# Block-sorted attention with a max-out layer behind it: the opening and the second batch's sorts in another order

## The chip, the cores and the metric

One core of one Trainium2 chip runs the whole program. The metric is the device time of one execution in microseconds (us); every number below is from the kernel before the change.

## What is computed

Inputs are q, k and v of shape 4 x 8 x 768 x 64 (batch, head, position, width), a sorting net of 4 x 8 x 8 x 8, and three weight matrices. Cut to what matters, the reference is:

```python
for _ in range(5):                       # Sinkhorn: P becomes a soft permutation of 8 blocks
    P = exp(P - max(P)); P /= sum(P, -1); P /= sum(P, -2)
k_sorted = einsum('bhij,bhjcd->bhicd', P, k_blocks)     # blocks of 96 positions
v_sorted = einsum('bhij,bhjcd->bhicd', P, v_blocks)
attn = softmax(q_blocks @ k_sorted.T / 8)               # inside each block
x = (attn @ v_sorted) as 3072 tokens x 512
out = maximum(x @ w1, x @ w2) @ w_out                   # d_ff = 1024
```

## The kernel before

**Stages.** The 32 Sinkhorn problems are done once, in small operations of VectorE (DVE) and ScalarE (ACT), while TensorE (PE) multiplies zeros (`keep_streaming`, line 77; the opening's call is line 666). The result is laid out as block-diagonal matrices (`block_diagonals`, line 293). Then, for each of the four batches:

- `sort_k` (line 385, three calls for a batch) and `sort_v` (line 409, four calls) multiply raw keys and values with those matrices; each has 16 or 32 small products in one PSUM tile, and one evacuation to SBUF. For batches 0 and 1 the values are first put into another order by `turn_v` (line 209, calls by columns 0 to 96), on ACT or DVE.
- `q_transposes` (line 349), in two halves. For batches 0 and 1 this is done by PE, for batches 2 and 3 by transposing DMAs of SyncE's queue (SP), after `pair_q` (line 339, DVE) has paired the heads. Half 0 holds head pairs 0 and 1, half 1 pairs 2 and 3.
- `scores` u = 0 to 7 (line 452): eight products and the exponential on ACT. u = 4·(half of the blocks) + head pair, so u = 0, 1, 4, 5 read q's half 0, and 2, 3, 6, 7 half 1.
- `values` u (line 480): eight products on PE, then on DVE a reciprocal (line 499) and a scaling (line 505) that writes x.
- `x_transposes` t = 0 to 3 (line 513), named TR in the text: t covers u = 2t and 2t + 1. For batch 0 it is done by PE and evacuated (`eng` says by which engine); for the other batches it is a transposing DMA on SP (line 518).
- the feed-forward layer: w1 is replaced by w1 - w2 in four column pieces (`w_difference`), since max(h1, h2) = relu(h1 - h2) + h2; `moe_h` (line 598) makes the relu part in eight steps for a batch, of which steps 0 to 3 read TR 0 and 1 and steps 4 to 7 read TR 2 and 3; within a step the head pairs come in the order 0, 2, 1, 3, and pairs 1 and 3 read the odd TR. `w2_transposes` and `w_product` make w2·w_out once. `moe_out` (line 627) makes the output for 128 tokens in two parts; after each second group of tokens one evacuation (128 x 1024 fp32) and one 512 KB write on SP.

**Order.** All engines run their instructions in the order in which the program issues them. The opening up to batch 0's attention is written out by hand (lines 666 to 722). Then a loop over batches runs a list of units (for batch 0: four `moe_h` of the first half, of which two are already done, four of the second, four `w_product`, twelve `moe_out` parts: units 0 to 23). After unit n it issues `tail[n]` (a table of extra steps by unit, lines 732 to 742), and then some of `steps`, the sorts and the attention of the next batch, spread from unit `lo` on in proportion to the units' costs. An evacuation without a named engine goes to ACT or DVE by `pick` (line 96), which keeps a running sum of the work given to each.

**Buffers and queues.** PSUM holds four tiles in rotation for everything; a product waits until one is free. All loads are issued by GpSimd's queue (POOL) with a cast from fp32 to bf16; q's raw tile has one buffer, so a load of q waits until the transposes or `pair_q` of the batch before have read it. Batch 2's load stands in `tail[14]`, batch 3's behind `pair_q(2)` in `tail[18]` (line 741).

Of the kernel before, what the change touches and what calls it, by code (L numbers as in the profile page):

```python
# [16 lines left out]
def kernel(  # L17
# [21 lines left out]
    B, H, S, D = q.shape  # L39
# [26 lines left out]
    def ps_f32(name):  # L66
        return psum.tile([128, 1024], FP32, tag="ps", name=name)

    def ps_bf16(name):
        return psum.tile([128, 2048], BF16, tag="ps", name=name)  # L70
# [6 lines left out]
    def keep_streaming(ps, n, by=None, most=512):  # L77

        w0 = fill[:, 0:128] if by is None else late[by]
        while n > 0:  # L80
            w = min(n, most)
            nc.tensor.matmul(ps[:, 0:w], w0, fill[:, 0:w], start=True, stop=True)  # L82
            n -= w
# [43 lines left out]
    for n in range(NE):  # L127
        t = big.tile([BLK, 8 * BLK + 32], BF16, tag=f"e{n}", name=f"e{n}")
# [16 lines left out]
    def load_k(b):  # L145
        k_raw[b] = kpool.tile([128, HB * D], BF16, tag="k_raw", name="k_raw")
        n = HB * D // NCH
        for ci in range(NCH):
            nc.gpsimd.dma_start(
                out=k_raw[b][:, ci * n : (ci + 1) * n],  # L150
                in_=k_src[b, :, ci * n : (ci + 1) * n],
            )

    def load_v(b, c0=0, pieces=2):
        r0 = (b % 2) * 64
        n = (BLK - c0) * D // pieces
        for m in range(pieces):
            nc.gpsimd.dma_start(
                out=v_raw[r0 : r0 + 64, c0 * D + m * n : c0 * D + (m + 1) * n],
                in_=v_src[b, :, c0 * D + m * n : c0 * D + (m + 1) * n],  # L160
            )
# [30 lines left out]
    def w_difference(t, eng=None):  # L192
        n = DFF // 4
        (eng or nc.vector).tensor_tensor(  # L194
            out=w1_sb[:, :, t * n : (t + 1) * n],
            in0=w1_sb[:, :, t * n : (t + 1) * n],
            in1=w2_sb[:, :, t * n : (t + 1) * n],
            op=ALU.subtract,
        )
        if not eng:  # L200
            load["D"] += 600

    w_difference(0, nc.gpsimd)
    w_difference(1, nc.gpsimd)
    load_v(1)
    load_k(1)


    def turn_v(rows, eng, c0, c1):
# [139 lines left out]
    def q_transposes(b, half, eng=None):  # L349

        if half == 0:
            qT[b] = qpool.tile([128, HP, R, 128], BF16, tag="qT", name="qT")
        if b > 1:
            hps = slice(half * 2, half * 2 + 2)
            nc.sync.dma_start_transpose(
                out=qT[b][:, hps].rearrange("p h r c -> p (h r) c"),
                in_=q_pair[b][:, hps].rearrange("p h r d -> p (h r d)"),
            )
            return
        ps = ps_bf16("tq_ps")  # L360
        if b == 0:
            nc.tensor.matmul(
                ps[:, 0:128], fill[:, 0:128], ident, is_transpose=True, start=True, stop=True
            )
        for n in range(2 * R):
            hp, r = half * 2 + n // R, n % R
            c = slice(n * 128, (n + 1) * 128)
            for h2 in range(2):
                nc.tensor.matmul(  # L369
                    ps[h2 * 64 : h2 * 64 + 64, c],  # L370
                    q_raw[b][:, hp + 4 * h2, r * D : (r + 1) * D],
                    ident,
                    is_transpose=True,
                    start=True,
                    stop=True,
                )
        evac(
            qT[b][:, half * 2 : half * 2 + 2].rearrange("p h r c -> p (h r c)"),
            ps[:, 0 : 2 * R * 128],
            2 * R * 128,  # L380
            two_x=True,
            eng=eng,
        )
# [274 lines left out]
    def att(b):  # L658

        SC = [lambda u=u: scores(b, u) for u in range(8)]  # L660
        VA = [lambda u=u: values(b, u) for u in range(8)]
        TR = [lambda t=t: x_transposes(b, t) for t in range(4)]
        return SC, VA, TR

    first, second, both = slice(0, 64), slice(64, 128), slice(0, 128)
    keep_streaming(ps_f32("fill_ps"), 88 * 138, most=138)
    for it in range(5):
        sinkhorn(it)
        if it < 2:
# [9 lines left out]
    turn_v(first, "D", 80, 96)  # L679

    SC, VA, TR = att(0)
    sort_k(0, 0, 2048, "A")
    sort_k(0, 1, 0, "D")
    sort_k(0, 2, 0, "A")
    sort_v(0, 0, 0, "D")
# [2 lines left out]
    sort_v(0, 2, 0, "A")  # L688
    sort_v(0, 3, 0, "D")
    SC[0]()  # L690
    SC[1]()
    q_transposes(0, 1, "D")
    SC[4]()
    VA[0]()
    scores(0, 2, 1024)
    VA[1]()
    SC[3]()
    values(0, 2, 1024)
    x_transposes(0, 0, "A")
    values(0, 3, 512)  # L700
    SC[5]()
    moe_h_products(0, 0, 0, (0, 2), 512)
    x_transposes(0, 1, "A")
    VA[4]()
    SC[6]()
    moe_h(0, 0, 0, "A", (1, 3))
    SC[7]()
    VA[5]()
    moe_h(0, 0, 1, "A")
    x_transposes(0, 2, "A")  # L710
    VA[6]()
    w_difference(2)
    VA[7]()
    w2_transposes(0, "D")()
    w_difference(3)
    for b in range(1, B):
        selections(b)
    for c, n, m in [(2, 1, 0), (3, 3, 1)]:
# [5 lines left out]
    def turn(rows, c0):  # L724
        turn_v(rows, "D", c0, c0 + 24)
        load["D"] += 850

    def load_rest():
# [1 line left out]
        load_k(2)  # L730

    tail = {
        2: [TR[3], lambda: w2_transposes(1, "A")(), load_rest],
        4: [lambda: turn(second, 0)],
        5: [lambda: block_diagonals([(0, 2), (1, 1), (1, 2), (1, 3)], 2)],
        6: [lambda: turn(second, 24), lambda: turn(second, 48)],
        7: [lambda: turn(second, 72)],
        8: [lambda t=t: sort_k(1, t) for t in range(3)],
        9: [lambda: load_v(2), lambda: load_v(3), lambda: load_k(3)],
        14: [lambda: load_q(2)],  # L740
        18: [lambda: pair_q(2, 0), lambda: pair_q(2, 1), lambda: load_q(3)],
# [1 line left out]
    for b in range(B):  # L743
        units = [lambda t=t: moe_h(b, 0, t, None if b else "A") for t in range(4)]
        if b == 0:
            units[0] = lambda: None
            units[1] = lambda: None
        units += [lambda t=t: moe_h(b, 1, t) for t in range(4)]
        cost = [13] * 8
        if b == 0:  # L750
            units += [lambda dmt=dmt: w_product(dmt) for dmt in range(4)]
            cost += [17] * 4
        units += [
            lambda ti=ti, part=part: moe_out(b, ti, part)
            for ti in range(6 if b < B - 1 else 4)
            for part in range(2)
        ]
        cost += [13] * 12
        if b == B - 1:
            units += [  # L760
                lambda: moe_out_last(4, [(0, 512, "D")]),
                lambda: moe_out_last(5, [(0, 384, "D"), (384, 512, "A")]),
            ]
        steps, lo = [], 0
        if b < B - 1:
            qs = [lambda half=half: q_transposes(b + 1, half) for half in range(2)]
            ks = [lambda t=t, b=b: sort_k(b + 1, t) for t in range(3)]
            SC, VA, TR = att(b + 1)

            def group(*fs):  # L770
                return [lambda: [f() for f in fs]]

            if b == 0:
                lo = 9
                vs = [lambda t=t: sort_v(1, t) for t in range(4)]
                for m, c in enumerate((0, 24, 48, 72)):
                    VA[m + 1 : m + 2] = group(VA[m + 1], lambda c=c: turn(both, c))
                steps = group(*vs[0:2]) + group(vs[2], qs[0]) + group(vs[3], qs[1])
            elif b == 1:
                vs = [lambda t=t: sort_v_pair(2, t) for t in range(8)]  # L780
                tail[0] = qs
                tail[10] = [lambda: pair_q(3, 0), lambda: pair_q(3, 1)]
                steps = group(*ks) + group(*vs[0:2]) + group(*vs[2:4]) + group(*vs[4:6])
                steps += group(*vs[6:8])
            else:
                tail[0] = qs
                lo = 4
                steps = group(*ks)
            steps += group(*SC[0:2]) + VA[0:1] + group(*SC[2:4]) + VA[1:2] + group(VA[2], TR[0])
            steps += group(*SC[4:6]) + VA[3:4] + group(VA[4], TR[1]) + group(*SC[6:8]) + VA[5:6]  # L790
            steps += group(VA[6], TR[2]) + group(VA[7], TR[3])
        done = 0
        for n, unit in enumerate(units):
            elapse(100 * cost[n] if n < len(cost) else 0)
            unit()
            for step in tail.get(n, []):
                elapse(250)
                step()
            total = sum(cost[lo:])
            want = -(-len(steps) * sum(cost[lo : n + 1]) // total)  # L800
            while done < min(want, len(steps)):
                elapse(250)
                steps[done]()
                done += 1
        tail = {}
# [28 lines left out]
```

## Time and profile before

| what | us |
|---|---|
| median of 3 runs (170.62 to 171.14) | 171.06 |
| the profiled execution | 170.89 |
| its span, first to last instruction | 169.0 |
| outside the span | 1.89 |
| PE busy | 161.8 |
| ACT busy | 85.8 |
| DVE busy | 75.8 |
| GpSimd busy | 28.6 |

The span lists PE, DVE and ACT work with start times; "busy" of PE includes the products of zeros. A waiting instruction shows the idle time before it and what released it. q0 is the queue of the loads that GpSimd issues, q1 that of the DMAs that SP issues (output writes and transposes). "To landing" is the time from a DMA's issue until all its data are in place.

Some matmul records are missing from the trace (a group of 8 is then shown as "x5" or "x7"), and the gap that this leaves is shown as "issue".

### The profile page before, as it was taken

What the parts mean: (1) busy time and instruction counts of PE and PEld (TensorE: products, weight loads), DVE (VectorE), ACT (ScalarE), POOL (GpSimd) and SP (SyncE); (2) the same over time, 40 slices, a digit from 0 to 9 for tenths busy, and PEclk for the clock granted to TensorE, in tenths of its full rate; (3) what the DMA queues carried; (4) which work ended last, traced back from release to release, by engine and by line L of the source; (5) the groups of instructions that cost most, each with busy time, mean ns of one, the idle gap of its engine ahead of it and who ended that gap; (6) DMA issues with size and microseconds to landing.
All of it is one profiled execution on the core that took longest, in us unless ns stands there. A gap on an engine that the chain in (4) does not pass through costs nothing.

```text
span 169.0 us, 4526 instructions
## 1 busy us (share of the span) xinstructions
PE 161.8 (96%) x2000; PEld 97.9 (58%) x2018; DVE 75.8 (45%) x174; ACT 85.8 (51%) x104; POOL 28.6 (17%) x44
## 2 busy tenths in 40 slices
PE   7999999999999999999999999999999999999991
PEld 7949676755764454566564545557545456654451
DVE  5968864948464459437743433205442160000011
ACT  3587878474674353176674505456615416642020
POOL 7865585223312003000000000000000000000000
PEclk9999999999999999999999999999999999999999
DMA  3999999999999994999700253690053255000333
GB/s 46 202 205 197 199 207 206 224 197 206 216 221 200 205 230 82 186 148 232 160 0 4 66 151 134 98 288 16 0 36 139 50 169 175 0 0 0 124 146 106
DMA packets 30243, 23.11 MB, mean 137 GB/s; under 512 B 16720, under 2 KB 25168, under 8 KB 30224
## 3 DMA queue, kind: packets, MB, share of 16 engines
q0 software_dynamic: 10880, 12.59, 44.8%
q1 hardware_dynamic: 19200, 10.17, 24.9%
q8 instruction: 16, 0.26, 0.6%
q10 hardware_dynamic: 144, 0.07, 0.1%
q14 instruction: 3, 0.02, 0.0%
HBM read 25.17 MB, written 6.29 MB: 186 GB/s over the span
## 4 chain that ended last, share of the span: by engine, by line
PE 92%; DVE 3%; issue 2%; ACT 1%
PE out_ps L617 35%; PE h_ps L590 25%; PE fill_ps L82 6%; PE o_ps L488 4%; PE wc_ps L570 4%; PE k_ps L394 4%; PE s_ps L461 4%; PE v_ps L415 2%; PE tq_ps L369 2%; PE v_ps L436 1%; PE tx_ps L526 1%; ACT v_sb L108 1%; DVE qT L110 1%; PE k_ps L82 1%; DVE q_pair L343 1%
## 5 line engine op out<-in xcount | busy, mean ns | idle before, releaser
L617 PE MATMUL out_ps<-wo_sb,g 128*128 128x512 bf16 (+2 forms) x188 | 47.0, 370 | 1.1 <-issue 0.3
L590 PE MATMUL h_ps<-xT,w_sb 128*128 128x384 bf16 x256 | 44.7, 326 | 0.6 <-ACT xT L108 0.4
L590 PEld LDWEIGHTS <-w_sb 128*128 128x128 bf16 x256 | 24.0, 98 | 16.4 <-DVE w_sb L194 0.4
L108 ACT COPY o<-out_ps 128x1024 f32<-128x1024 f32 x11 | 11.1, 1012 | 40.4 <-issue 22.8
L604 ACT ACTIVATE g<-h_ps 128x768 bf16<-128x768 f32 x27 | 21.9, 812 | 16.7 <-PE h_ps L590 16.7
L469 ACT ACTIVATE e<-s_ps 96x768 bf16<-96x768 f32 x32 | 24.2, 804 | 6.3 <-PE s_ps L461 6.3
L617 PEld LDWEIGHTS <-g 128*128 128x128 bf16 x200 | 16.9, 97 | 15.7 <-DVE x L505 0.4
L617 PE MATMUL out_ps<-wc,xT 128*128 128x512 bf16 (+2 forms) x100 | 24.8, 370 | 0.1
L505 DVE TENSOR_TENSOR x<-o_ps,rs 96x512 bf16<-96x512 f32 x32 | 22.0, 686 | 1.1
L499 DVE RECIPROCAL rs<-o_ps 96x8 f32<-96x8 f32 x32 | 6.5, 202 | 34.0 <-PE o_ps L488 33.8
L617 PEld LDWEIGHTS <-xT 128*128 128x128 bf16 x100 | 9.6, 97 | 11.2
L488 PEld LDWEIGHTS <-e 96*128 96x128 bf16 x256 | 11.7, 98 | 6.0 <-ACT e L469 0.2
L488 PE MATMUL o_ps<-v_sb,e 96*128 96x65 bf16 x256 | 12.9, 193 | 0.0
L652 DVE COPY o<-out_ps 128x512 f32<-128x512 f32 (+1 forms) x2 | 1.2, 625 | 25.0 <-PE out_ps L617 25.0
L110 DVE CAST kT<-k_ps 128x1024 bf16<-128x1024 f32 x5 | 6.0, 1223 | 12.3 <-PE k_ps L394 12.3
L110 DVE CAST v_sb<-v_ps 96x1024 bf16<-96x1024 f32 x8 | 9.6, 1216 | 2.8 <-PE v_ps L415 1.7
L461 PEld LDWEIGHTS <-kT 64*128 64x128 bf16 x256 | 6.1, 94 | 6.2 <-issue 5.4
L108 ACT CAST v_sb<-v_ps 96x1024 bf16<-96x1024 f32 x8 | 8.0, 1006 | 3.2 <-PE v_ps L415 1.9
L136 POOL DMA_DIRECT2D q_raw<-in_q_dram x7 | 6.4, 936 | 18.7 <-DVE rs L499 14.0
L82 PEld LDWEIGHTS <-fill 128*128 128x128 bf16 x98 | 8.5, 122 | 1.6 <-DVE fill L73 1.2
L461 PE MATMUL s_ps<-qT,kT 64*128 64x96 bf16 x256 | 8.9, 204 | 0.4 <-DVE qT L110 0.2
L82 PE MATMUL fill_ps<-fill 128*128 128x138 bf16 x88 | 7.9, 274 | 1.2 <-DVE fill L73 1.2
(77 smaller groups left out, 137.5 us busy)
## 6 DMA issues: line engine op xcount, KB each, us to landing
out_dram<-o SPq DMA_DIRECT2D x11, 512.0 KB, 3.1
k_raw<-in_k_dram POOLq DMA_DIRECT2D x12, 256.0 KB, 12.2
v_raw<-in_v_dram POOLq DMA_DIRECT2D x6, 384.0 KB, 12.5
q_raw<-in_q_dram POOLq DMA_DIRECT2D x3, 768.0 KB, 11.5
w_sb<-in_moe_w_dram POOLq DMA_DIRECT2D x4, 256.0 KB, 9.9
w_sb<-in_moe_w_dram POOLq DMA_DIRECT2D x2, 512.0 KB, 11.2
wo_sb<-in_moe_w_out_dram POOLq DMA_DIRECT2D x2, 512.0 KB, 14.9
v_raw<-in_v_dram POOLq DMA_DIRECT2D x3, 256.0 KB, 4.9
```

Source lines behind the costliest of these rows:

```text
L82: nc.tensor.matmul(ps[:, 0:w], w0, fill[:, 0:w], start=True, stop=True)
L108: nc.scalar.copy(out=out_ap, in_=in_ap)
L110: nc.vector.tensor_copy(out=out_ap, in_=in_ap)
L394: nc.tensor.matmul(ps[r0 : r0 + 64, m * 64 : (m + 1) * 64], kv[r0 : r0 + 64, t * 16 + m, :], bd_k[b][r0 : r0 + 64, :], start=True, stop=True,)
L461: nc.tensor.matmul(ps[:, h2 * 512 + ii * 128 : h2 * 512 + ii * 128 + BLK], kT[b][rows, (hp * 8 + i) * BLK : (hp * 8 + i) * BLK + 128], rhs ...
L469: nc.scalar.activation(out=e[:, 0 : 8 * BLK].rearrange("p (t c r) -> p t c r", t=8, r=R), in_=ps[0:BLK] .rearrange("p (t f) -> p t f", t=8 ...
L488: nc.tensor.matmul(ps[:, h2 * 512 + ii * 65 : h2 * 512 + (ii + 1) * 65], e[:, (h2 * 4 + ii) * BLK : (h2 * 4 + ii) * BLK + 128], v_sb[:, m0 ...
L505: nc.vector.tensor_tensor(out=x, in0=ov[:, :, :, 0:D], in1=rs.to_broadcast([BLK, 2, 4, D]), op=ALU.mult,)
L570: nc.tensor.matmul(ps[:, 0:512], w2T[:, fb, dmt * 128 : (dmt + 1) * 128], wo_sb[:, fb, :], start=(fb == 0), stop=(fb == NFB - 1),)
L590: nc.tensor.matmul(h_ps[t][:, m * 512 : m * 512 + TCH], w1_sb[:, hp, fb * 128 : (fb + 1) * 128], xT[:, b % 2, ch, hp % 2, hp // 2, :], sta ...
L604: nc.scalar.activation(out=g, in_=src, func=AF.Relu)
L617: nc.tensor.matmul(dst, g_tiles[b, ch, m // 2][:, m % 2, off : off + 128] if m < NFB else xT[:, b % 2, ch, hp % 2, hp // 2, off : off + 12 ...
```

## The change

It has two groups of edits.

In the opening: q's half 1 is transposed directly behind `scores` 0 instead of behind `scores` 1; `scores` 4 moves from behind them to behind `x_transposes(0, 0)`; the second `x_transposes` is evacuated by DVE instead of ACT; `values` 5 stands ahead of `scores` 7; `w_difference(3)` stands ahead of the evacuation of the first `w2_transposes`. The zero products ahead of `sort_k(0, 0)` go from 2048 columns to 1024, ahead of `scores` 2 from 1024 to 512; one product of zeros ahead of q's half 1 goes; the opening's 88 products of 138 columns become 86 of 142.

In the second batch: its keys are loaded ahead of its values; its three `sort_k` move from `tail[8]` to `tail[7]` with fixed engines and with the value turns between and behind them; its `sort_v` and `q_transposes` leave `steps` for `tail[9]` to `tail[11]`; `lo` goes from 9 to 12, so `steps` begins with `scores` 0 and 1. The second `w2_transposes` and the loads of `load_rest` move from `tail[2]` to `tail[3]`.

```diff
-    load_v(1)
     load_k(1)
+    load_v(1)
...
-        if b == 0:
+        if b == 0 and half == 0:
...
-    keep_streaming(ps_f32("fill_ps"), 88 * 138, most=138)
+    keep_streaming(ps_f32("fill_ps"), 86 * 142, most=142)
...
-    sort_k(0, 0, 2048, "A")
+    sort_k(0, 0, 1024, "A")
...
     SC[0]()
+    q_transposes(0, 1, "D")
     SC[1]()
-    q_transposes(0, 1, "D")
-    SC[4]()
     VA[0]()
-    scores(0, 2, 1024)
+    scores(0, 2, 512)
     VA[1]()
     SC[3]()
     values(0, 2, 1024)
     x_transposes(0, 0, "A")
+    SC[4]()
     values(0, 3, 512)
     SC[5]()
     moe_h_products(0, 0, 0, (0, 2), 512)
-    x_transposes(0, 1, "A")
+    x_transposes(0, 1, "D")
     VA[4]()
     SC[6]()
     moe_h(0, 0, 0, "A", (1, 3))
+    VA[5]()
     SC[7]()
-    VA[5]()
...
-    w2_transposes(0, "D")()
+    w2T_ready = w2_transposes(0, "D")
     w_difference(3)
+    w2T_ready()
...
     tail = {
-        2: [TR[3], lambda: w2_transposes(1, "A")(), load_rest],
-        4: [lambda: turn(second, 0)],
+        2: [TR[3]],
+        3: [lambda: w2_transposes(1, "A")(), load_rest],
         5: [lambda: block_diagonals([(0, 2), (1, 1), (1, 2), (1, 3)], 2)],
-        6: [lambda: turn(second, 24), lambda: turn(second, 48)],
-        7: [lambda: turn(second, 72)],
-        8: [lambda t=t: sort_k(1, t) for t in range(3)],
+        7: [
+            lambda: sort_k(1, 0, 0, "A"),
+            lambda: turn(second, 0),
+            lambda: turn(second, 24),
+            lambda: sort_k(1, 1, 0, "A"),
+            lambda: sort_k(1, 2, 0, "D"),
+        ],
+        8: [lambda: turn(second, 48), lambda: turn(second, 72)],
         9: [lambda: load_v(2), lambda: load_v(3), lambda: load_k(3)],
         14: [lambda: load_q(2)],
         18: [lambda: pair_q(2, 0), lambda: pair_q(2, 1), lambda: load_q(3)],
...
             if b == 0:
-                lo = 9
+                lo = 12
...
-                steps = group(*vs[0:2]) + group(vs[2], qs[0]) + group(vs[3], qs[1])
+                tail.update({9: vs[0:2] + tail[9], 10: [vs[2], qs[0]], 11: [vs[3], qs[1]]})
```

More of the change, by code (lines that the diff above doesn't have):

```diff
@@ L204 @@
     w_difference(1, nc.gpsimd)
+    load_k(1)
     load_v(1)
-    load_k(1)
     def turn_v(rows, eng, c0, c1):
```

## Prediction

> **What bounds the kernel now.** I read the busy line and the chain first, then the waits of PE, then the opening, then SP's queue against the loads.
>
> ```profile
> PE 161.8 (96%) x2000; PEld 97.9 (58%) x2018; DVE 75.8 (45%) x174; ACT 85.8 (51%) x104; POOL 28.6 (17%) x44
> PE 92%; DVE 3%; issue 2%; ACT 1%
> ```
>
> PE is the bound and its work is in a fixed order, so only three things change the time: products of zeros, waits of PE, and new waits. The waits of PE between 12 and 72.6 us (engine, line, releaser: total, times, longest):
>
> ```profile
> PE h_ps L590 <- ACT xT L108: 0.4, 1, 0.4
> PE out_ps L617 <- DVE x L505: 0.3, 1, 0.3
> PE h_ps L590 <- DVE w_sb L194: 0.3, 1, 0.3
> PE s_ps L461 <- DVE qT L110: 0.2, 1, 0.2
> ```
>
> From 72.6 us to the end the same view lists none. So there is about 1.2 us of waits to win, and some zeros. In the opening, q's half 1 arrives late and scores 2 wait for it (timeline: start, duration):
>
> ```profile
> 18.34 0.86 PE L369 MATMUL tq_ps<-ident,q_raw 128*64 128x128 bf16 x24
> 19.24 0.96 DVE L110 COPY qT<-tq_ps 128x1536 bf16<-128x1536 bf16 x1 [0.42 <-PE tq_ps L369]
> 20.25 0.60 PE L461 MATMUL s_ps<-qT,kT 64*128 64x96 bf16 x8 [0.21 <-DVE qT L110]
> ```
>
> Now batch 1's TR, which the change delays. SP's queue (TR 1 at 64.11; TR 2 and 3 from 69.36), POOL's load of q for batch 3, and how long a DMA took to land: TR 1 took 2.8 us, TR 2 8.6 us.
>
> ```profile
> 64.11 1.22 SPq L518 DMA_TRANSPOSE xT<-x  x1
> 67.03 0.38 SPq L637 DMA_DIRECT2D out_dram<-o  x1
> 69.36 4.80 SPq L518 DMA_TRANSPOSE xT<-x  x2
> 66.07 1.77 POOL L136 DMA_DIRECT2D q_raw<-in_q_dram  x1 [13.99 <-DVE rs L499]
> xT<-x SPq DMA_TRANSPOSE x1, 2.8
> xT<-x SPq DMA_TRANSPOSE x1, 8.6
> ```
>
> The reason for 8.6 us is in the packets between 71 and 74 us: q0 (the load) moves, q1 (SP's DMAs) all but stands still.
>
> ```profile
> q0 software_dynamic: 626, 0.48, 120.1%
> q1 hardware_dynamic: 22, 0.01, 1.5%
> ```
>
> The first q0 packets of that load come in the slice from 69 us, about 3 us after its issue; it lands after 11.5 us, at 77.6; TR 2 lands at 69.36 + 8.6 = 78.0, just behind it. Nobody needs TR 2 before 81.9, so this costs nothing now.
>
> **What the Trainium skill says.** "DMA: Bandwidth & Descriptors", section "Queues, rings and completion order", says that a DMA engine takes turns between the queues, one packet each, and that one queue's descriptors go in order on each engine. The trace is harsher on the first point (626 packets to 22), and agrees with the second as far as it shows. Even fair turns would not help: the load has about 1,010 packets, a transpose about 800, so it would take most of the load's 7.5 us. "TensorE: Matmul & The Clock Gate", section "Part 1: The HAM clock gate", says that PE's clock halves after an idle window of some 3.4 us. No wait in this trace is that long; it bears on one rival below.
>
> **The change, part by part.**
>
> *Zeros.* Four products of 512 ahead of sort_k 0 become two: 4 x 0.21 us run from 11.80 to about 12.66, but the block diagonal ends near 12.73 and the sort starts at 12.83. So at most 0.05 us is won; I take 0.05. The zero product ahead of q's half 1 goes (0.06, inside the next sum). 86 x 142 against 88 x 138 columns is 0.6% of a 7.9 us row: 0 to +0.05 us, taken as 0.
>
> *q's half 1.* Behind scores 0 (one set is 0.27 us, from 17.58) its transposes run 17.84 to 18.63, since they take the PSUM tile that half 0's copy left at 17.53. DVE is busy with the last value sort to 18.82, then copies (0.96) to 19.78, not 20.20. Scores 2 start at 19.83: 0.42 us earlier. But scores 4 (0.27 us) filled that wait and now run later, and one zero product less (0.21) had filled it too, so behind values 3 PE is only 0.15 us ahead. Values 0 and scores 1 fit without a wait; counting tiles against their releases I find a free one each time.
>
> *TR 1 of batch 0 on DVE.* ACT takes 0.80 for this copy. DVE's rows give 0.96 for 1536 and 1.21 for 2048 columns, so by their slope 0.59 for 768 (between 0.5 and 0.8). It ends at 25.25 (ACT: 25.63), moe_h goes on at 25.30 instead of 25.68: 0.38 us ahead. Values 5 ahead of scores 7 is order alone. DVE now has to do rs 4 and x 4 (0.9) behind the copy, which end at 26.2 and are read at 27.9: hidden.
>
> *w_difference.* Piece 2 is released by rs and x of values 6, which move 0.38 earlier with PE, so the wait at 30.62 stays, 0.38 earlier. Piece 3 (0.68) ahead of the w2T copy ends at 31.7, needed at 31.9. The w2T copy (1.2) has until 39. So the **opening gives 0.38 + 0.05 = 0.43 us** (0 to 0.6).
>
> *Keys first, sorts earlier.* Loads run back to back: the second piece of wo lands at 33.2. Keys then land by 37.1 (sorts need them from 39.8), values at 39 and 41 (before: 35.2 and 37.4). The four turns (0.83 each) and one kT copy (1.22) fill DVE from 39.4 to about 44.2; sort_v needs them at 44.7. Covered with 0.5 us; were it gone, each turn late costs up to 0.83. POOL issues the second half of batch 3's values behind the last turn, at 44.2 instead of 42.0; its turn in the queue is near 53, so the stream has no hole and batch 2's q still lands at 62.7. The second w2 transposes and load_rest one unit later: w2T's copy ends at 36.0, read at 39; 0.
>
> *One unit later.* Batch 1's scores, values and TR now come a whole unit (1.3 us) later against moe_out and tail[18]. This has two effects. At 66.3 PE now waits 0.3 us for x of values 4, which stood behind pair_q in DVE's queue; with values 3 behind pair_q instead, two more tiles are free at that point: **-0.3 us**. The other effect is on TR 1. With moe_out of unit 19 ending at 65.2 (0.43 earlier gives 52.2 for unit 12, then eight units of 1.3, three score pairs of 0.45 and four values of 0.25):
>
> - DVE: pick now gives it the first output copy (its sums are 0.30 + 1.02 on ACT against 0 + 1.20), 58.85 to 60.05 by the 1.22 us row of the same size. Then rs, x (0.9), turn (0.8), rs, x, turn: 63.4. pair_q twice (1.0): 64.4. POOL issues batch 3's q 0.3 later: **64.7**.
> - x of values 3 is behind pair_q: 65.35. TR 1 stands in SP's queue behind the output write of unit 19 (copy 65.3 to 66.3 on ACT, issue 0.4): **66.75**. Before, it was 2 us ahead of the load; now it is 2 us behind it, and behind 512 KB of output.
> - The load's packets begin near 67.7 and it lands at 64.7 + 11.5 = 76.2; TR 1 lands about 0.4 later, at 76.6, as TR 2 does now.
> - moe_h of batch 1 is reached at 65.2 + 6.65 = 71.9 and reads TR 1 after two products, at 72.2. **PE waits 4.4 us**, with everything behind it on PE: nothing else is queued that could run. Afterwards TR 2 and 3 and q's transposes have landed in time, since moe_h 4 and scores of batch 2 come later too.
>
> Bounds: if the output write too is held, TR 1 lands up to 1.4 us later (5.8); if part of TR 1 gets through first, the wait is 0 to 2.
>
> **Sum.** -0.43 - 0.3 + 4.4 = +3.7 us on the profiled execution's 170.89 (169.0 span and 1.89 around it): **174.6**. That execution is 0.17 below the median of the runs shown, within their spread.
>
> **Rivals.**
>
> - *TR 1 is not caught* (faster). It decides whether TR 1's packets are through before the load's begin: the load's issue must come after about 66, that is DVE 1.3 us later than I have it, or the engines must take short packets first. Then the wait is 0 and the time is 170.89 - 0.73 = 170.2. For it: TR 1 took 2.8 us with the queue free. Against it: TR 2, TR 3 (6.2) and the first q transpose (7.7) were all held by this load.
> - *The wait also cools the clock* (slower still). 4.4 us is longer than the window that the skill's page gives. The opening shows a slow stretch of about 5 us at 115 ns for a zero product where later 60 is seen; half of 4 to 5 us is 2 to 2.5 us: 176.8. Against it: the window may not fall into the wait.
> - *Nothing measurable*: TR 1 gets through and the opening's 0.4 us is eaten by turns that come late or by a tile that is given out in another order: 170.9.
>
> **How the numbers follow.** Held TR 1 at the full clock 0.55, held and cooled 0.18, not caught 0.18, nothing measurable 0.09. About 0.3% (0.5 us) is what a measurement of this kernel can tell from no change. Slower 0.73, same 0.09, faster 0.18. The slower cases alone reach from 172.5 to 178; to leave out no more than 2 in 10, the range starts at the faster case, 170.2, and ends at 177.6.
>
> **What would show it.** Right: a wait of 4 us of `h_ps L590` near 72 us, released by a DMA of xT; TR 1's landing time at 9 to 10 us; POOL's load of q issued ahead of it. In the opening, qT's copy directly behind v_sb's, and h_ps waiting for a DVE xT. Wrong: TR 1 landing in about 3 us or the load issued behind it; then the kernel is faster. A wait of sort_v for v_dc near 45 would show the turns uncovered.

## The result, and the profile after

Changed kernel: 176.76 us (175.79 to 176.81, 4 runs), beside 170.84 for the one before on the same chip; ratio 1.034, 95% interval 1.029 to 1.038. It is 5.9 us slower. The profiled execution took 176.71 (span 174.8, mean clock of PE 0.978).

The busy line, the clock in 40 slices and the chain of the changed kernel:

```profile
PE 163.4 (93%) x1994; PEld 99.1 (57%) x2012; DVE 75.9 (43%) x174; ACT 85.4 (49%) x104; POOL 28.6 (16%) x44
PEclk9999999999999999956999999999999999999998
PE 84%; DVE 6%; DMA 6%; issue 2%; ACT 0%
```

PE is busy 1.6 us longer although it has fewer products, a DMA has entered the chain with 6% of the span, and in two slices, from 74 to 83 us, the clock is low. The waits of PE over the whole span name the DMA:

```profile
PE h_ps L590 <- DMA xT<-x: 4.3, 1, 4.3
PE fill_ps L82 <- DVE fill L73: 1.2, 1, 1.2
PE k_ps L394 <- DVE bd L321: 0.4, 1, 0.4
PE s_ps L461 <- DVE qT L110: 0.4, 1, 0.4
PE h_ps L590 <- DVE w_sb L194: 0.3, 1, 0.3
PE out_ps L617 <- issue: 0.2, 1, 0.2
```

The waits for xT from ACT (0.4) and for x of values 4 (0.3) are gone, and one of 4.3 us has come. It is batch 1's first moe_h, after two products. The timeline shows POOL's load, SP's queue and PE at that place (the second transpose of the third line is TR 2):

```profile
64.80 1.77 POOL L136 DMA_DIRECT2D q_raw<-in_q_dram  x1 [11.09 <-DVE rs L499]
66.70 0.39 SPq L637 DMA_DIRECT2D out_dram<-o  x1
67.13 5.69 SPq L518 DMA_TRANSPOSE xT<-x  x2
72.17 0.49 PE L590 MATMUL h_ps<-xT,w_sb 128*128 128x384 bf16 x2
76.99 2.08 PE L590 MATMUL h_ps<-xT,w_sb 128*128 128x384 bf16 x6 [4.33 <-DMA xT<-x]
79.00 2.74 PE L394 MATMUL k_ps<-bd,k_raw 64*64 64x64 bf16 x96
81.67 0.50 PE L590 MATMUL h_ps<-xT,w_sb 128*128 128x384 bf16 x2
```

The load is issued 2.3 us ahead of TR 1 (before: 2.0 us behind it). In the DMA view the output write of 66.70 took 8.7 us to land, and TR 1 9.8 us. Packets between 68 and 71 us, by queue:

```profile
q0 software_dynamic: 539, 0.41, 106.1%
q1 hardware_dynamic: 3, 0.01, 0.6%
```

The load has the DMA engines for itself while two of SP's DMAs are queued. This holds for the first part of the load only: from 71 us on, packets of both queues move side by side, as between 72 and 73 us:

```profile
q0 software_dynamic: 95, 0.07, 46.3%
q1 hardware_dynamic: 100, 0.20, 60.0%
```

What moves there is the output write; TR 1's own packets follow behind it, from about 74 us. The clock, in stretches of 2 us (each line: stretch, its length, busy time and count of PE, PEld, DVE, ACT, POOL, then granted clock, DMA share, GB/s):

```profile
72.00:74.00 2.00, 0.66 (x11) 0.37 (x10) 0.89 (x2) 1.01 (x1) 0.00 (x0) 1.00 1.16 280
74.00:76.00 2.00, 0.00 (x0) 0.00 (x0) 0.00 (x0) 0.00 (x0) 0.00 (x0) 0.69 1.39 121
76.00:78.00 2.00, 1.01 (x4) 0.49 (x4) 0.00 (x0) 0.00 (x0) 0.00 (x0) 0.50 1.17 329
78.00:80.00 2.00, 2.00 (x42) 1.20 (x42) 0.00 (x0) 0.81 (x1) 0.00 (x0) 0.50 1.22 296
80.00:82.00 2.00, 2.00 (x70) 1.84 (x65) 1.04 (x1) 1.22 (x2) 0.00 (x0) 0.60 1.13 255
```

The clock falls to half during the wait and stays there for some 4.6 us of work after it, to 81.6. So the span divides as follows. PE reaches moe_h 0.42 us earlier (72.17 against 72.59); it goes on at 76.99 where before the same product ran at 72.92, +4.07; from there to the next moe_h it needs 4.68 us instead of 2.70, +1.98; the rest to the end is 0.25 us shorter. Together this is +5.8, the difference of the spans.

### The profile page after: what moved, and what is told of

The parts are those of the page before. It is cut to its first block, busy times and chain, and to the rows that moved or that the text cites. A ratio compares the mean times of both kernels' runs of the same rounds, so it can differ in the third digit from the quotient of the medians.

```text
span 174.8 us, 4515 instructions
## 1 busy us (share of the span) xinstructions
PE 163.4 (93%) x1994; PEld 99.1 (57%) x2012; DVE 75.9 (43%) x174; ACT 85.4 (49%) x104; POOL 28.6 (16%) x44
## 4 chain that ended last, share of the span: by engine, by line
PE 84%; DVE 6%; DMA 6%; issue 2%; ACT 0%
PE out_ps L617 30%; PE h_ps L590 25%; PE fill_ps L82 6%; DMA xT<-x 6%; PE k_ps L394 4%; PE wc_ps L570 4%; PE s_ps L461 3%; PE o_ps L488 3%; PE v_ps L415 2%; DVE v_dc L217 2%; PE tq_ps L369 1%; PE v_ps L436 1%; PE tx_ps L526 1%; DVE o L110 1%; DVE v_sb L110 1%
## 5 line engine op out<-in xcount | busy, mean ns | idle before, releaser
L590 PE MATMUL h_ps<-xT,w_sb 128*128 128x384 bf16 x256 | 45.9, 331 | 4.7 <-DMA xT<-x 4.3
L108 ACT COPY o<-out_ps 128x1024 f32<-128x1024 f32 x10 | 10.1, 1012 | 36.0 <-issue 19.8
L82 PE MATMUL fill_ps<-fill 128*128 128x142 bf16 x86 | 8.0, 277 | 1.2 <-DVE fill L73 1.2
## 6 DMA issues: line engine op xcount, KB each, us to landing
q_raw<-in_q_dram POOLq DMA_DIRECT2D x3, 768.0 KB, 11.6
```

The lines of the kernel that those rows point to most:

```text
L108: nc.scalar.copy(out=out_ap, in_=in_ap)
L590: nc.tensor.matmul(h_ps[t][:, m * 512 : m * 512 + TCH], w1_sb[:, hp, fb * 128 : (fb + 1) * 128], xT[:, b % 2, ch, hp % 2, hp // 2, :], sta ...
```

## Experiments

Theory A: the load's packets hold SP's DMAs, so TR 1 lands with the load; the wait is 4.3 us and the clock behind it costs 2 us more. The rivals are: B, the later sorts and DVE's fuller queue; C, the output write ahead of TR 1; D, the 2 us lie in the key sort and not in the clock; E, the opening loses too. Medians stand beside those of the kernel before in the same comparison, ratios with their 95% interval.

**TR 1 ahead of the write**, for batch 0's loop only:

```diff
-            steps += group(*SC[4:6]) + VA[3:4] + group(VA[4], TR[1]) + group(*SC[6:8]) + VA[5:6]
+            steps += group(*SC[4:6]) + group(VA[3], *([] if b else TR[1:2]))
+            steps += group(VA[4], *(TR[1:2] if b else [])) + group(*SC[6:8]) + VA[5:6]
```

> The changed kernel with batch 1's TR 1 put directly behind values 3 instead of values 4, so that it stands ahead of the output write in SP's queue; nothing else moves, the load of batch 3's q keeps its place. Theory A (SP's DMAs are held while that load's packets run): TR 1 is issued near 65.4 instead of 67.1, its packets run before the load's begin near 67, it lands in 3 to 4 us, PE doesn't wait for xT, 170.4 us. Rival B (the loss lies in the later sorts and DVE's fuller queue, TR 1 only comes last by chance): TR 1 is late again or another wait of 3 us or more takes its place, 175 us or more. Theory A with the bound that TR 1 itself needs the DMA engines until 68: up to 2 us of wait, 172.

170.15 us (before 170.62), ratio 0.998 (0.997 to 0.999). One place in one queue wins back all 6 us; B falls, since the sorts, DVE and PE kept their order. TR 1 was issued at 65.93, 0.6 us behind the load, and landed after 6.2 us, not 3 to 4: at 72.1, about 1 us ahead of its reader. 768 of its 800 packets had moved by 69 us; the last ones came during the load. So it got through, but only just.

**The load two units later**, SP's order untouched:

```diff
-        18: [lambda: pair_q(2, 0), lambda: pair_q(2, 1), lambda: load_q(3)],
+        20: [lambda: pair_q(2, 0), lambda: pair_q(2, 1), lambda: load_q(3)],
```

> The changed kernel with the two pair_q of batch 2, and with them the load of batch 3's q that waits for them, two units later (behind unit 20 instead of 18). SP's order is untouched: the output write still stands ahead of TR 1. Theory A: the load is issued near 69, its packets begin near 72, TR 1 (issued near 67.1) lands by 71.5, no wait of PE for xT, clock full all the time: 170.4 us, and the first kernel here that may beat the one before (by 0.3%). Rival C (the output write ahead of TR 1 in the same queue is what holds it): TR 1 lands near 76 as in the changed kernel, 176 us. Rival B: 175 us or more.

170.82 us (170.62), ratio 1.002 (1.000 to 1.004). The load was issued at 68.59, and TR 1 behind the same write landed after 6.0 us, at 72.9. The wait is nearly gone:

```profile
PE h_ps L590 <- DMA xT<-x: 0.5, 1, 0.5
```

C, as the main cause, falls: the write is still ahead of TR 1. But TR 1 was 1.4 us later than I had expected, and 0.5 us of wait stayed. The write's data don't explain that: 0.50 of its 0.52 MB had moved by 68.75 us. Between 69.75 and 71.25 us SP's queue moved only 29 packets, and the load's first packets came later, at 71.4. What stopped it there isn't shown.

**TR 1 one step later in the kernel before**, again for batch 0's loop only:

```diff
-            steps += group(*SC[4:6]) + VA[3:4] + group(VA[4], TR[1]) + group(*SC[6:8]) + VA[5:6]
+            steps += group(*SC[4:6]) + VA[3:4] + group(VA[4], *(TR[1:2] if b else []))
+            steps += group(*SC[6:8], *([] if b else TR[1:2])) + VA[5:6]
```

> The kernel before with one edit: batch 1's TR 1 one step later, behind scores 6 and 7, so that in SP's queue it comes behind the output write and, at about 67.4 us, 1.3 us behind the issue of the load of batch 3's q. All other engines keep their order. Theory A: TR 1 lands with the load near 77.9, PE waits at 72.9 for some 5 us, the clock drops afterwards for some 5 us (2 us lost): 177.7 us. Rival B (the order of the sorts makes the loss): 170.9 us, no wait.

178.35 us (170.62), ratio 1.046 (1.040 to 1.051). The same wait and the same drop of the clock, without any other edit of the change; the loss is 7.7 us, since TR 1 landed after 10.9 us:

```profile
PE h_ps L590 <- DMA xT<-x: 5.3, 1, 5.3
PEclk9999999999999999987999999999999999999999
```

**Zeros in the wait.** The changed kernel, with products of zeros for 4.05 us ahead of batch 1's first moe_h:

```diff
-        units = [lambda t=t: moe_h(b, 0, t, None if b else "A") for t in range(4)]
+        units = [
+            lambda t=t: moe_h(b, 0, t, None if b else "A", n=19 * 512 if (b, t) == (1, 0) else 0)
+            for t in range(4)
+        ]
```

> The changed kernel with 19 zero products of 512 columns (4.05 us at full clock) on PE ahead of batch 1's first moe_h, where it waits for TR 1. The wait's end is set by the DMA, so the zeros cost nothing as long as they are over by then. Theory A with the clock's part (4.3 us of wait and about 2 us of half clock behind it): the clock stays full, 176.8 - 2.0 = 174.7 us. Rival D (the time beyond the wait is lost elsewhere, in the key sort of batch 2 or in its evacuations): 176.8 us.

174.41 us (170.62), ratio 1.022 (1.018 to 1.026). The loss is 3.8 us where the changed kernel lost 5.9, so 2.1 us less, with more work on PE, and the clock is full in all slices. TR 1 is as late as before (9.9 us), and the wait left behind the zeros is 0.3 us. D falls; the clock's part is shown.

**Issue or packets?** The kernel before, with pair_q and the load behind unit 17:

```diff
-        18: [lambda: pair_q(2, 0), lambda: pair_q(2, 1), lambda: load_q(3)],
+        17: [lambda: pair_q(2, 0), lambda: pair_q(2, 1), lambda: load_q(3)],
```

> The kernel before with the two pair_q of batch 2, and the load of batch 3's q behind them, one unit earlier (behind unit 17, so ahead of values 3 in DVE's order). SP's order stays: TR 1 with no output write ahead of it. By DVE's rows the load is then issued near 64.1 us and TR 1 near 64.7, so the load is issued first, as in the changed kernel, but its packets begin only some 3 us later, near 67. Theory A in its narrow form (what counts is whose packets run first, not whose issue): TR 1's packets run from 65.6 to 67.4, it lands by 68, no wait, 170.6 us. Theory A' (once the load is issued ahead, TR 1 is held, whatever stands between): TR 1 lands near 75.5, PE waits some 2.5 us, 173.5 us or more.

170.41 us (170.61), ratio 0.997 (0.996 to 0.999). The load is now issued ahead of TR 1 (63.73 against some 64.3), and PE doesn't wait for xT. The packets of the stretches 65 to 66 us (first line), 66 to 67 (two lines) and 68 to 70 (two lines) show why:

```profile
q1 hardware_dynamic: 293, 0.08, 40.9%
q1 hardware_dynamic: 475, 0.12, 59.4%
q0 software_dynamic: 18, 0.01, 30.1%
q0 software_dynamic: 432, 0.33, 122.3%
q1 hardware_dynamic: 32, 0.00, 2.2%
```

768 of TR 1's 800 packets run in the 3 us that the load needs here between its issue and its packets. It landed after 5.8 us, at 70.1, not by 68, since the last 32 packets moved only during the load. So the narrow form of A holds for the wait and missed the landing by 2 us. The wait of 0.3 us at values 4 is gone, as the prediction said of pair_q ahead of values 3.

**Each group of edits alone.** First the opening of the changed kernel with everything else as before, then the second batch's edits with the opening as before.

> Only the first group of edits: the opening of the changed kernel (q's half 1 behind scores 0, scores 4 later, a DVE copy for the second transposes, fewer zeros, w_difference 3 ahead of the copy of w2T), with the loads and the second batch's sorts of the kernel before. Theory A: the opening gives what its trace showed from the first block-diagonal product on, 0.3 us, and TR 1 keeps its place: 170.3 us, ratio 0.998. Rival E (the opening loses as well, which the wait hides): 171.2 us or more.

170.43 us (170.61), ratio 0.998 (0.997 to 1.000): no loss, a gain at the edge of what can be told.

> Only the second group of edits: keys loaded first, sorts and value turns in fixed places, steps from unit 12 on, with the opening of the kernel before. Theory A: the whole loss is here: the wait for TR 1 (4.3 us) and the half clock behind it (2.0 us), against 0.2 us won at values 4: 176.9 us. Rival E (part of the loss is in the opening): 175.5 us or less.

177.43 us (170.61), ratio 1.037 (1.033 to 1.042), 0.5 us above the expectation; the wait is 4.6 us, and TR 1 landed after 10.1 us. The whole loss is in the second group; E falls.

**Fewer zeros in the opening**, on top of TR 1 ahead of the write:

```diff
-    keep_streaming(ps_f32("fill_ps"), 86 * 142, most=142)
+    keep_streaming(ps_f32("fill_ps"), 78 * 142, most=142)
```

> The changed kernel with TR 1 behind values 3, as before, and the opening's zero products cut from 86 to 78. The products of zeros end near 11.7 us while the Sinkhorn result is there at 11.25. If they bound the opening, 8 of them (0.06 us each at full clock, 0.12 at half) are 0.5 us, of which at most 0.45 can be won before the Sinkhorn result binds: 169.8 us, ratio 0.995. If the clock comes to full speed later by as much, or the result isn't ready, nothing is won: 170.2 us.

171.03 us (170.61), ratio 1.004 (1.002 to 1.006), worse than either case expected. The first block-diagonal product did start earlier, at 11.44 instead of 11.88. But PE then stood still inside scores 3, with nothing that released it:

```profile
PE s_ps L461 <- issue: 1.0, 1, 1.0
```

Four of its 22 executions took 172.2 to 173.1 us with a mean clock of 0.978 to 0.990, where the kernel before never shows less than 0.996. That looks like a TR 1 that was caught after all, but these four were not the profiled one, so it isn't shown.

**Combinations.** The opening with the load behind unit 17, and TR 1 ahead of the write with the load behind unit 20:

> The opening of the changed kernel (first group of edits alone) with the two pair_q of batch 2 behind unit 17 instead of 18: the two edits that each won a little alone (170.43 and 170.41 against 170.61 and 170.6). If they add up, as they lie in different stretches: the wait of 0.3 us at values 4 goes too, TR 1's packets run ahead of the load's or with their beginning, no wait for xT: 170.0 us, ratio 0.996. If the earlier opening brings the load's packets ahead of TR 1's, a wait for xT comes: 172 us or more.

170.13 us (170.55), ratio 0.997 (0.996 to 0.999). Whether the two gains add can't be told from these intervals. Here the load was issued at 63.63 and its first packets came after only 1.6 us, ahead of TR 1's, which was issued at 64.55 with no output write ahead of it. The packets between 65 and 69 us:

```profile
q0 software_dynamic: 729, 0.56, 105.6%
q1 hardware_dynamic: 1, 0.00, 0.0%
```

So TR 1 was held whole, and C isn't needed for it. The expected 172 us didn't come, because the load itself landed after 8.7 us instead of 11.6; TR 1 landed after 8.4 us, at 72.95, which is just about when moe_h reads it. This version stands on the edge of the same wait.

> The changed kernel with both cures: TR 1 directly behind values 3 in SP's queue, and pair_q with the load of batch 3's q behind unit 20. TR 1 has the queue for itself and lands in 3 to 4 us, near 68.5; no wait for xT. Theory A: 170.2 us as with the first cure alone, since the second has nothing left to win. If pair_q ahead of values 3 costs PE something by holding x, 170.0; if pair_q behind unit 20 holds x of values 5 and a PSUM tile with it, up to 170.8.

170.14 us (170.55), ratio 0.997 (0.995 to 0.998). TR 1 landed after 2.8 us, and PE's waits behind 12 us are 0.4, 0.2 and 0.2. It is 0.3% faster than the kernel before and, of the two combinations, the one with room around TR 1.

## Why the prediction was right, and what it mis-sized

- **The cause was right**: pair_q and the load come ahead of values 3 and TR 1, TR 1 stands behind the write, lands with the load, and PE waits. Load issued at 64.80 (said: 64.7), TR 1 at 67.13 (66.75), landing after 9.8 us (9 to 10), moe_h reached at 72.17 (71.9), wait 4.33 (4.4). That the wait fits within 0.1 us is in part luck, for both of its ends came 0.3 to 0.5 us later than said: the terms listed for the end of unit 19 add up to 64.95, not 65.2, and it came at 65.6. The load has 1,040 packets, not 1,010; nothing hangs on that. Both directions were shown: one edit to the changed kernel takes the wait away, one edit to the kernel before makes it.
- **The clock was the term that was mis-sized.** The sum counted the wait at full clock, 174.6, and gave "the wait also cools the clock" (2 to 2.5 us, 176.8) 0.18. The runs showed the drop: all twelve executions of the three kernels whose profile shows a wait of 4.3 us or more have a mean clock of 0.971 to 0.990. Its price in the changed kernel was 2.0 us by the trace and 2.1 by the run with zeros. The Trainium skill ("TensorE: Matmul & The Clock Gate", section "Part 1: The HAM clock gate") gives about 3.4 us for the window. The traces do not bear this figure out as a time from the last product. The stretches in which the clock fell, in the changed kernel, in the kernel before with TR 1 late and in the second group alone (granted clock third from the end):

```profile
74.50:75.00 0.50, 0.00 (x0) 0.00 (x0) 0.00 (x0) 0.00 (x0) 0.00 (x0) 0.76 1.58 120
77.50:78.00 0.50, 0.00 (x0) 0.00 (x0) 0.00 (x0) 0.00 (x0) 0.00 (x0) 0.95 1.34 104
78.50:79.00 0.50, 0.50 (x5) 0.29 (x3) 0.00 (x0) 0.00 (x0) 0.00 (x0) 0.95 1.04 406
```

From the shares (full clock is 1.00, half 0.50), the clock fell at about 74.76, 77.95 and 78.95, which is 2.1, 4.9 and 5.3 us after PE's last product, and in the third case 0.7 us after PE had gone on. The first of these is shorter than the page's window, and the measurement decides: the moment varies. So does the work that half clock covered: 4.6, 2.9 and 3.4 us of PE's time. But each of these waits brought a drop, so with hindsight the drop belonged in the sum.
- **The opening**: -0.43 was expected up to moe_h of batch 0, and 0.33 measured (from the first block-diagonal product to w_difference 2: 18.25 us before, 17.92 after). The 0.05 for zeros ahead of the key sort wasn't there: that sort now waits for the block diagonal (0.4 us) and starts 1.19 us behind the first product, as before. qT's copy directly behind v_sb's and the DVE copy of 0.56 us (said: 0.59) came as predicted:

```profile
17.67 1.22 DVE L110 CAST v_sb<-v_ps 96x1024 bf16<-96x1024 f32 x1
18.83 0.96 DVE L110 COPY qT<-tq_ps 128x1536 bf16<-128x1536 bf16 x1
19.84 0.35 PE L461 MATMUL s_ps<-qT,kT 64*128 64x96 bf16 x8 [0.40 <-DVE qT L110]
24.81 0.56 DVE L110 COPY xT<-tx_ps 128x768 bf16<-128x768 bf16 x1 [0.67 <-PE tx_ps L526]
```

- **Values 4**: the 0.3 us wait went, as said. Yet PE reached batch 1's moe_h only 0.42 us earlier, not 0.7. In this trace 0.07 of that was lost ahead of the first block-diagonal product, where the traces differ by up to 0.7 us (11.32 to 12.03): the opening's zeros run at about 11 in a us at first and at some 20 later, and the change had come by the sixth us in the trace with 11.32 and not before the eighth in the one with 12.03. Another 0.1 is what the opening gave less than said; the rest was not traced to one place.
- **The covers held**: turns, values and w2T made nobody wait; sort_v started at 45.02, 0.6 behind the last turn.

## What to carry to other kernels

When steps are shifted against each other by one unit, follow every DMA that they issue against the large loads of another queue, not only the engines' work: the load here was never waited for, but what it held was. A transfer that someone waits for should have its packets through before a bulk load's packets begin, and the cheap cure is its place in its own queue. Where a forecast wait of PE is as long as those that dropped the clock here (4.3 us and more), the price of the slow stretch behind it belongs in the sum.

## What the runs showed of the hardware

- The Trainium skill ("DMA: Bandwidth & Descriptors", section "Queues, rings and completion order") says that a DMA engine takes turns between queues by packet. Here, from 68 to 71 us, q0 moved 539 packets and q1 three, with two DMAs of SP waiting; from 72 to 73 us it was 95 and 100, which looks like turns. A transpose that takes 2.8 us alone took 9.8 to 10.9 us. Why no turns are seen in the load's first part stays open, and so does whether the packets of the profile are those of that page.
- A load of 768 KB by GpSimd had its first packets 1.6 to 3.6 us after its issue in the twelve traces, and landed after 8.0 to 12.1 us. A transpose issued within 1 us behind it got nearly all of its packets through where the load took 2.9 us to start, and none where it took 1.6. What sets this time wasn't tested.
- The granted clock of the profile reads 1.00 all through the opening, although the zero products there run at about half their later rate at first (11 in a us, later 20). So that figure did not show this slow stretch.
- PE can stand still for 0.2 us (first group alone) to 1.0 us (fewer zeros) between two products of one small group near 20 us, with no releaser shown; the place moves by a few products between the kernels here, and some kernels with the new opening, the changed one among them, show no such stop. With 8 zero products fewer it was longest, and the one packet of the instruction queue of that stretch came between 19 and 20 us instead of 18 and 19. That PE ran out of instructions there is a guess; no run tested it.
